# The opening of a written-out instruction order, exchanged for another

## The chip, the cores and the metric

The kernel runs on one core of a Trainium2 chip. The metric is the device time of one execution in microseconds (us). A core has TensorE (PE, matmuls; PEld is its weight load), VectorE (DVE), ScalarE (ACT), GpSimd (POOL) and SyncE (SP), which here does nothing but issue transfers. Each engine works its own instructions in program order, and waits at semaphores for the others.

## The reference, cut to what matters

A recurrence over 768 steps with a 40x40 state for each of 4 batches and 8 heads, and behind it an MLP with a quick GELU over the 3072 tokens of its output. All is float32.

```python
for t in range(S):                       # r, k, v, w, a, b: (4, 8, 768, 40)
    y[:, :, t] = einsum('bhd,bhde->bhe', rt, state)
    Sa = einsum('bhde,bhe->bhd', state, at)
    state = state * wt[:, :, None, :] - einsum('bhd,bhe->bhde', Sa, bt) \
            + einsum('bhd,bhe->bhde', vt, kt)
...
x = y.transpose(0, 2, 1, 3).reshape(3072, 320)
h = x @ w_in                             # 320 -> 2048
out = (h / (1 + exp(-1.702 * h))) @ w_out   # 2048 -> 320
```

## The kernel before

The 768 steps are cut in 12 chunks of 64, and the 4 batches in 2 pairs: 24 *units*, numbered in pairs, units 2c and 2c+1 being the two batch pairs of chunk c. Each unit is worked in the same stages. A name with a number is that stage of that unit (N0, N1):

- loads by SP: `logw`, `ak` (a and k side by side), `b`, `rv`, `RV`, `time`, and from unit 4 on `wc`. `ak`, `b` and `rv` are two transfers each, of 40 partitions; the others one of 128;
- the logarithm of the decay on ACT (L526), its sums over time on PE (`cum`, `cumc`), the exponentials FT, GT and G on ACT (L565 to L591), and a and b, k scaled with them (`ahT` L619, `bhT` L621, `khT` L624, `kh` and `bh` L627, on DVE or POOL);
- scores on PE: A and RV, and N, which needs ahT and bhT;
- the inverse of (1 - N), by five *levels* of squaring (`plain_level` for units 0 to 3): matmuls into `ps_level`, a copy of the result to PT (L784, "PT" or "PV") on ACT or DVE, a transpose to EX (L723) on DVE, then the next level. Behind the fifth a transpose (ES, L702), its spread into T (L707 on ACT, L709 on POOL), and two small steps Q and T21;
- the solution X, masked into M (L907, DVE), and y with the new state (`ps_y`, L934 to L945). For units from 2 on, the state of two units before enters (zr, zT, rz);
- x, y scaled by FT (L953), goes to DRAM and comes back turned as xT (L963, L967).

When both units of a chunk are done, its MLP follows: `up` (40 tasks of 8 matmuls in four groups, up0 to up3), GELU to g on ACT (L988), and `down` (2 x 8 tasks of 16 matmuls).

The MLP's weights come as 8 pieces of four transfers of 320 KB each (`wt0` to `wt7`; `extra`, part of `w_sb` or of `xT_all` hold them meanwhile), in a 64-bit form. One step on ACT (`rebased`, L447), three on DVE (L451, L455, L459) and one on POOL (L463, 3 us) turn a piece to float32. Pieces 0 to 3 serve up0 to up3, and 4 to 7 serve `down`. Piece 5 may be loaded when piece 0 is done, 6 after 3, and 7 after 5.

The work is kept as 2700 numbered tasks. No planner runs at build time: a string, `ORDER`, lists the tasks in the order in which they are issued, each as number, engine letter (p PE, a ACT, d DVE, g POOL, s SP) and, for work on PSUM, one of four bank pairs. `listed` reads it and checks each task's forerunners. Several tasks can run on either of two or three engines; the letter decides. What the order doesn't say, semaphores do: a task waits on its engine for its inputs and free buffers, and all behind it on that engine waits with it. That holds for SP too.

Of the kernel before, what the change touches and what calls it, by code (L numbers as in the profile page):

```python
# [58 lines left out]
class Plan:  # L59
# [29 lines left out]
    def listed(self, text):  # L89

        assert len(text.split()) == len(self.tasks)
        table, out, done = "exp", [], set()
        for one in text.split():
            e = next(e for e in ENGINES if ENGINES[e] in one)
            n, bank = one.split(ENGINES[e])
            t = self.tasks[int(n)]
            assert e in t.engines and t.after <= done and (e == "SP" or (t.pair is None) == (not bank))
            t.engine, t.bank = e, int(bank or 0)
            if e == "ACT" and t.table:
                t.load, table = t.table != table, t.table  # L100
            done.add(t)
            out.append(t)
        return out
# [4 lines left out]
0s 8s 26s 5s 7s 9s 3a 6s 87p0 88p1 24s 89a1 1s 2s 12s 102a 95d 100p2 90a0 93d 158a 101d2 98p3 96g 10s 94d 17s 97g 16s 99d3  # L108
103p1 4a 11s 132p0 104a1 105d1 142p2 143p3 133a0 106d 130p1 14s 144a3 13s 107p0 15s 18s 151g 108a0 109d0 51s 131a1 110p3 27s
149g 150d 111a3 112d3 159p0 156p1 145a2 161d0 160a0 152g 113p3 345s 92a 162d 25s 153d 114a3 163p2 42s 115d3 34s 19a 274s 264p0  # L110
165d2 265p3 164a2 22d 266a3 166p2 20d 273s 21d 33s 43s 167a2 154p3 168d2 23g 35s 28a 157d1 116p2 155d3 169p1 117a2 118d2 267a0
279d 63s 280g 119p3 277s 171d1 36s 44s 123a3 120d3 343s 125d3 121a 278g 124d3 29d 287a 126p2 170a1 288p0 127a2 30d 172p1 479s
122a3 31d 289a0 128p2 54s 173a1 45s 129d2 32g 62s 174d1 134p3 37a 290d0 175p2 344s 135d3 180a2 146s 178a2 275s 176d2 136p1
179a2 38d 181a2 39d 177a 282g 276s 291d 91s 138a1 182p0 188p3 281d 183a0 186p2 139d 137a1 283p0 187a2 184p1 189a3 40d 140s
292p2 46a 60s 284d0 41g 285p3 185d1 148a 286d3 190p0 293a2 294d2 334p1 335p3 357a 191d0 141s 268g 147s 336a3 315d 192p2 47d
337a1 348d 316p0 194a2 346s 295p3 349d 61s 317a0 195g 347s 358p1 296a3 297d3 360d1 318a0 298p3 271a 361d 319p0 338g 300d3 196s
193a2 320a0 355p2 385d 270s 48d 299a3 362p0 356d2 351g 301p3 363a0 364d0 350g 386p2 197s 302d3 365p0 387a2 269s 352g 359a1
303d3 388a2 323p1 367d0 366a0 321p3 49d 324a1 304p2 322a3 478s 325d1 50g 353p0 309a2 470p3 354d0 209p1 307a2 210p1 310a2 305d2
211p1 308a2 272d 198p0 341a 199p0 72s 212p1 70s 64a 200p0 340s 368p2 52s 342d 339s 69s 201p0 369a2 202p0 370d2 203p0 471a
213p1 65d 214p1 389p2 66d 472a3 483g 204p0 390a2 560s 371p3 67d 306a 53s 215p1 71s 482s 216p1 372a3 217p1 476a 220p2 373d3 68g  # L120
218p1 221p2 477d 219a1 205p0 222p2 206p0 223p2 224p2 78s 559s 207p0 55a 311p3 225p2 79s 312d3 80s 226p2 208a0 58d 313p1 374p3
314d1 227p2 56d 379a3 228p2 229p2 57d 326p0 230a2 59g 393p1 327d0 378a3 391p2 394a1 375d3 231p0 558s 392d2 376a 232p0 233p0
395d1 81s 73a 234p0 480s 381p2 235p0 474s 328p1 475s 382a2 74d 377a3 485d 380a3 236p0 75d 481s 492a 242p2 486d 243p2 82a 76d
484d 77g 383p3 237p0 384d3 244p2 329d1 330d1 488p3 473d 238p0 531d 245p2 487g 246p2 489d3 85d 532p1 708s 239p0 533a1 396p3
331d 534a1 240p0 247p2 397d3 332s 241a0 562s 535p1 83d 490p3 536a1 84d 398p0 706s 572a 491d3 86g 550p1 253p3 399d0 551a 555s
400d0 561s 333s 254p3 401d 255p3 552a1 564d 493p0 402s 556a 567g 570p1 554s 494d0 248p2 705s 563d 566g 249p2 495d0 498d 256p3
571d1 565g 403s 250a2 496a0 251d2 696p1 497g 557d 539p0 252s 537p2 257p3 538a2 704s 540d0 701s 258p3 553d 611d 697a 499d 573p2
259p3 576a2 574d2 784s 710d 700s 260p3 787s 541d0 575d2 404p0 578d 261a3 577g 405p0 579d 698a1 568p2 711g 500p1 406p0 569d2
501a1 407p0 262d3 580p2 702a 502d1 263s 408p0 582d2 409p0 503d 410p0 583d 504a 612p3 411p0 584g 613d3 412p0 614d3 413p0 505p1
709d 414a0 426p3 506d1 427p3 428p3 507d1 429p3 699d 581d2 430p3 615p1 703d 431p3 616a1 785s 585p0 432p3 508d 586a0 433p3 587d0  # L130
434p3 509a 588d 435p3 589d 448p2 436a3 510p1 590p0 511a1 449p2 592d0 591a0 512d1 415p3 513d 416p3 593d 514a 417p3 594g 418p3
515p0 419p3 516a0 517d0 595p1 518d 420p3 596a1 597d1 421p3 598d 422p3 519a 599d 423p3 424p3 520p0 425a3 437p1 521d0 438p1
523d0 522g 439p1 524d0 440p1 525d0 441p1 442p1 526d0 527p3 718p0 528a3 443p1 719d0 929s 444p1 720d0 529p3 445p1 721d0 446p1
530d3 600p0 723d 447a1 542p3 722d 724g 603d0 605a0 619p1 604d0 543d3 450p2 620a1 606d0 544p3 621d1 601d0 602d 617p1 707s 546d3
451p2 618a1 783s 712d 547g 713d 607p0 725p1 608a0 452p2 609p0 453p2 548s 610d0 932s 454p2 727d1 726d1 622p0 728d 545d3 729a
775p1 455p2 623d0 780s 776a 549s 756d 730p3 624p0 456d2 457d2 731d3 458s 459p2 777a1 778g 732d3 786s 788g 781a 779s 626d0
460p2 625d0 627g 733d 795p1 835d 734a 461p2 735p3 791g 462p2 628s 736a3 796d1 737d3 716p0 792g 738d 463p2 782d 739g 1011s
920p1 757p3 925s 464p2 717d0 758a3 629s 759a3 790d 465p2 740p0 789d 466p2 741a0 742d0 921a 797p3 467d2 760p0 1008s 468d2 800a3
923d 652p2 469s 761d0 922a1 653p2 926a 930s 798d3 714p1 799d3 654p2 924s 802d 801g 655p2 934d 803a 656p2 836p0 657p2 715d1
658p2 659p2 837d0 762p3 838d0 927d 660p2 763a3 661p2 764p1 662a2 743d 630p0 744d 928s 631p0 632p0 765d1 804p3 766d1 633p0  # L140
805a3 806d3 634p0 807d 635p0 808a 745p2 636p0 748d2 637p0 749d2 839p1 933g 750d2 638p0 840a1 1009s 751d2 639p0 809p3 746d2
935g 640a0 641p1 810d3 642p1 793p2 747a 811d3 674p0 812d 794d2 813a 752p3 643p1 753a3 814p2 644p1 815a2 816d2 754p3 645p1
755d3 646p1 817d 647p1 818a 767p2 841p3 768d2 648p1 842a3 649p1 819p2 650p1 820a2 821d2 769p3 822d 651a1 823d 675p0 771d3 931s
770d3 772g 824p2 936d 676p0 827a2 828a2 942p1 829a2 677p0 1153s 830a2 937d 945a1 773s 663p3 825d2 664p3 943d1 1156s 826a 665p3
944d1 999p2 947d 946g 666p3 1000a 1004s 980d 940p1 948g 667p3 941d1 668p3 774s 669p3 670p3 831p1 671p3 1001a2 1002d 1003s
832d1 672p3 1005a 1013d 678p0 673a3 1006d 833p2 843p1 679p0 834d2 1007s 844d1 938p2 845d1 680p0 939d2 846p3 681p0 847d3 949p1
1012g 682d0 848p2 950a1 683d0 1014d 684s 685p3 849d2 1015g 1010s 850d2 1021p0 1016g 951d1 686p3 1024a0 1232s 851d 1235s 981p2
687p3 982a2 952d 852s 1022d0 983a2 953g 1144p1 1023d0 688p3 1026d 1145a 1149s 1025d 1027g 984p2 1059d 689p3 1154s 954p0 853s
985a2 1147g 690p3 1158d 1148s 955a0 956d0 986p2 1146a1 957d 1150a 691p3 958d 987a2 1151d 988p0 692p3 989a0 1152s 990d0 959p1
693a3 865p2 960a1 694d3 866p2 961d1 867p2 695s 962d 868p2 963d 1028p0 869p2 1029a0 1030d0 870p2 1031d 1157g 871p2 1159d 1032a  # L150
1060p3 872p2 873p2 1061a3 874p2 1062d3 1033p1 875a2 854p0 1035d1 855p0 1036d 856p0 1037d 1063p3 857p0 1064d3 1034a1 858p0
964p2 859p0 965a2 966d2 1038p1 967d 860p0 1039a1 1040d1 861p0 1041d 1017p3 968a 1042g 862p0 1018d3 863p0 969p2 864a0 876p1
970d2 877p1 972d2 971g 1043p3 973d2 878p1 1044a3 974d2 879p1 975d2 880p1 881p1 1045d3 1019p0 1046d 976p2 1047a 882p1 1020d0
1233s 883p1 977a2 1166p3 884p1 1169a3 1167d3 1377s 978p0 885p1 1168d3 898p2 1171d 1170g 886a1 979d0 887p3 1172a 1048p0 991p1
1051a0 888p3 1052a0 992d1 889p3 1053a0 890p3 1054a0 891p3 1049d0 993p1 1050a 1067p0 994d1 1160g 1155s 892p3 1161d 1068a0 893p3
894p3 1069d0 1380s 895p3 1204d 1065p0 995d1 896p3 996d 1066a0 1231s 1055p1 899p2 897a3 1056d1 997s 1173p0 1223p3 900p2 1174a0
# [973 lines left out]
```

## Time and profile before

| | |
|---|---|
| times of three runs | 684.27, 674.71, 680.40 us; median 680.40 |
| profiled execution | 682.79 us, its span 681.1 us |
| granted clock of PE, mean | 0.99 |
| busy, share of the span | PE 96%, DVE 65%, ACT 49%, POOL 26% |
| transferred | 69.73 MB, of which 21.63 MB in the first 100 us |

The span runs from the first to the last instruction; 1.7 us lie around it. A row of the timeline gives start, length, engine, source line, operation, what it writes and reads, and in square brackets the idle time of the engine before it with what ended that. L300 is the helper of all matmuls, so matmuls are told apart by their PSUM tile: `ps_N`, `ps_level`, `ps_y`, `ps_up`.

### The profile page before, as it was taken

Reading aid. Unit: us, or ns where it says so; the run is one execution under the profiler, and the core shown is the slowest. Engines: PE = TensorE matmul, PEld = TensorE weight load, DVE = VectorE, ACT = ScalarE, POOL = GpSimd, SP = SyncE. Lnnn points to the kernel's source line nnn. Section 1 sums busy time; section 2 is a strip of 40 time slices with the busy share of each in tenths; the row PEclk is TensorE's granted clock in tenths of the full one; section 3 lists DMA queues with packets and bytes.
Section 4 is the critical chain, followed back from the end, with each engine's and each line's share of the span. In section 5 each row is a group of like instructions: output and inputs, shape, how many; then the busy total and the mean of one; then the engine's idle time right before and its main releaser. Section 6 shows DMA issues by size and latency. Waiting matters only on the chain.

```text
span 681.1 us, 42181 instructions
## 1 busy us (share of the span) xinstructions
PE 652.0 (96%) x19488; PEld 572.4 (84%) x19488; DVE 445.5 (65%) x906; ACT 330.7 (49%) x688; POOL 176.7 (26%) x204
## 2 busy tenths in 40 slices
PE   5777999999999999999999999999999999999997
PEld 5667888997987788888888898899899799889996
DVE  4687877777867668767776587868556766675001
ACT  4675845544564654664545445455454354252110
POOL 5443444225123123123123211321412421300000
PEclk9788999999999999999999999999999999999999
DMA  7874755205314314432404413513502312200100
GB/s 235 275 244 148 228 158 173 89 14 155 108 50 139 103 45 125 124 108 67 121 23 131 140 34 107 154 33 106 149 29 71 121 51 58 58 13 23 51 12 21
DMA packets 35312, 69.73 MB, mean 102 GB/s; under 512 B 5440, under 2 KB 14656, under 8 KB 35136
## 3 DMA queue, kind: packets, MB, share of 16 engines
q1 hardware_dynamic: 35136, 67.03, 32.8%
q8 instruction: 153, 2.51, 1.6%
q14 instruction: 23, 0.19, 0.1%
HBM read 59.15 MB, written 7.86 MB: 98 GB/s over the span
## 4 chain that ended last, share of the span: by engine, by line
PE 91%; DMA 4%; ACT 1%; DVE 1%; issue 1%; SPq 0%; ACTq 0%; DVEq 0%
PE ps_up L300 31%; PE ps_down L300 30%; PE ps_level L300 9%; PE ps_y L300 5%; PE ps_B L300 4%; PE ps_X L300 2%; PE ps_N L300 2%; PE ps_rz L300 2%; PE ps_RV L300 2%; PE ps_A L300 1%; DMA ak<-in_ak 1%; PE ps_zT L300 1%; PE ps_Q L300 1%; DMA time<-in_time 1%; PE ps_T L300 1%
## 5 line engine op out<-in xcount | busy, mean ns | idle before, releaser
L300 PE MATMUL ps_up<-xT_all,w_sb 64*64 64x256 f32 x3840 | 254.4, 377 | 2.0 <-DMA xT_all<-x_dram 1.1
L300 PE MATMUL ps_down<-w_sb,g 64*64 64x320 f32 x3072 | 240.3, 430 | 1.1 <-issue 0.9
L300 PEld LDWEIGHTS ps_up<-xT_all,w_sb 64*64 64x64 f32 x3840 | 172.9, 133 | 17.7 <-issue 2.5
L300 PEld LDWEIGHTS ps_down<-w_sb,g 64*64 64x64 f32 x3072 | 143.3, 133 | 31.4 <-issue 1.6
L988 ACT ACTIVATE g<-ps_up 128x1024 f32<-128x1024 f32 x48 | 49.1, 1024 | 44.7 <-PE ps_up L300 44.3
L709 POOL TENSOR_TENSOR EX<-ES,quads 128x512 f32<-128x512 f32 x29 | 38.3, 1323 | 115.5 <-DVE ES L702 83.1
L751 ACT COPY W<-ps_level 128x512 f32<-128x512 f32 x56 | 32.7, 585 | 69.1 <-PE ps_level L300 67.4
L300 PEld LDWEIGHTS ps_level<-W,EX 64*64 64x64 f32 x2560 | 59.2, 134 | 5.8 <-DVE T L830 0.2
L300 PE MATMUL ps_level<-W,EX 64*64 64x64 f32 (+1 forms) x2560 | 56.2, 217 | 0.0
L753 DVE TENSOR_TENSOR E<-two,ps_level 128x256 f32<-128x256 f32 x80 | 33.1, 415 | 34.7 <-ACT W L751 30.7
L707 ACT ACTIVATE EX<-ES,quads 128x256 f32<-128x256 f32 x80 | 36.3, 501 | 30.4 <-DVE ES L702 29.9
L619 POOL TENSOR_TENSOR ak<-ak,FT 128x512 f32<-128x512 f32 x16 | 22.0, 1378 | 76.2 <-DMA ak<-in_ak 54.4
L300 PE MATMUL ps_level<-PT,EX 64*64 64x64 f32 (+2 forms) x1280 | 34.9, 244 | 5.7 <-DVE EX L723 4.8
L300 PEld LDWEIGHTS ps_level<-PT,EX 64*64 64x64 f32 x1280 | 32.6, 145 | 8.9 <-DVE EX L723 5.7
L702 DVE STREAM_TRANSPOSE ES<-E 128x256 f32<-128x256 f32 x80 | 35.2, 442 | 4.7 <-DVE E L753 0.5
L300 PE MATMUL ps_y<-M,bh 64*64 64x104 f32 (+1 forms) x768 | 34.8, 247 | 1.3 <-DVE M L907 0.8
L300 PE MATMUL ps_y<-RV,kh 64*64 64x104 f32 (+1 forms) x768 | 34.9, 247 | 0.3 <-DVE EX L723 0.3
L891 ACT COPY B<-ps_B 128x416 f32<-128x416 f32 (+1 forms) x34 | 16.5, 492 | 33.5 <-PE ps_B L300 33.2
L300 PEld LDWEIGHTS ps_y<-RV,kh 64*64 64x64 f32 x768 | 28.9, 133 | 2.0 <-DVE M L907 0.5
L907 DVE TENSOR_TENSOR M<-ps_X,later 128x832 f32<-128x832 f32 (+1 forms) x24 | 23.8, 993 | 9.8 <-PE ps_X L300 9.5
L627 POOL TENSOR_TENSOR kh<-time,G 128x320 f32<-128x320 f32 x18 | 16.2, 902 | 48.4 <-PE ps_y L300 34.4
L300 PEld LDWEIGHTS ps_y<-M,bh 64*64 64x64 f32 x768 | 27.0, 133 | 1.9 <-DVE M L907 1.2
(131 smaller groups left out, 1097.2 us busy)
## 6 DMA issues: line engine op xcount, KB each, us to landing
ak<-in_ak SPq DMA_DIRECT2D x48, 160.0 KB
rv<-in_rv SPq DMA_DIRECT2D x48, 160.0 KB
time<-in_time SPq DMA_DIRECT2D x24, 320.0 KB
xT_all<-x_dram SPq DMA_DIRECT2D x48, 160.0 KB
wc<-in_wc SPq DMA_DIRECT2D x20, 264.0 KB
logw<-in_w SPq DMA_DIRECT2D x24, 160.0 KB
RV<-in_v SPq DMA_DIRECT2D x24, 160.0 KB
b<-in_b SPq DMA_DIRECT2D x48, 80.0 KB
```

The lines of the kernel that those rows point to most:

```text
L300: nc.tensor.matmul(o, lhsT, rhs, start=start, stop=True, skip_group_check=True)
L619: plan.add(R, {"DVE": 690.0, "POOL": 1270.0, "sbuf": True}, lambda t: of(t.engine).tensor_mul(ahT(), ahT(), FT_of(i)), reads=T("ak", "FT") ...
L627: plan.add(R + 4, {"POOL": 870.0, "DVE": 490.0, "sbuf": True}, lambda t, n=n, dst=dst: of(t.engine).tensor_mul(dst(i)[:, :, :D], by_head(t ...
L702: plan.add(rank, dve(256), lambda t: nc.vector.transpose(ES(n), source(t)), writes=[key("ES", n, 6)], **reads)
L707: nc.scalar.activation(dst[:, :, h], ES(n), ACT.Copy, scale=quads[:, h, :1])
L709: of(t.engine).tensor_mul(dst, ES(n).unsqueeze(2).to_broadcast([128, 8, 2, 32]), quads.unsqueeze(1).to_broadcast([128, 8, 2, 32]))
L751: plan.add(rank, any2(512), lambda t: copy(t.engine)(tiles_of(W(n + 1)), blocks(psum(t, ""), 64)), writes=[key("W", n + 1, 5)], pair=pair)
L753: plan.add(rank, dve(256), lambda t: nc.vector.tensor_sub(tiles_of(E(n + 1)), every(two32, [128, 2, 4, 32]), blocks(psum(t, ""), 64)[:, :, ...
L891: plan.add(R, any2(4 * wide), lambda t: copy(t.engine)(dst(), some(psum(t, "")[:, :, :208])), writes=[("Bv", i)] if x and c > 0 else T("B" ...
L907: plan.add(R + 1, dve(8 * wide), lambda t: nc.vector.tensor_tensor(M_of(i)[:, :, :wide].rearrange("p (j b) n -> p b j n", b=2), some(psum( ...
L988: plan.add(-45, {"ACT": 1030.0, "table": "gelu"}, lambda t: nc.scalar.activation(g_of(c * NQ + q).rearrange("p m r n -> p r m n"), psum(t, ...
```

## The change

`ORDER` is exchanged for another list of the same 2700 tasks, and `listed` stores for SP's tasks an attribute `window`, which nothing else reads. Matmuls, copies and transfers are the same in number and shape. The lists differ in their first parts: the first 163 of PE's 1080 tasks, and the first 95 of SP's 268. Behind that each engine has its tasks in the same order, with bank pairs 0 and 2 exchanged. 37 tasks have another engine: DVE has 796 tasks for 785, ACT 418 for 433, POOL 138 for 134.

```diff
             assert e in t.engines and t.after <= done and (e == "SP" or (t.pair is None) == (not bank))
             t.engine, t.bank = e, int(bank or 0)
+            if e == "SP":
+                t.window = t.bank
...
-0s 8s 26s 5s 7s 9s 3a 6s 87p0 88p1 24s 89a1 1s 2s 12s 102a 95d 100p2 90a0 93d 158a 101d2 98p3 96g 10s 94d 17s 97g 16s 99d3
-103p1 4a 11s 132p0 104a1 105d1 142p2 143p3 133a0 106d 130p1 14s 144a3 13s 107p0 15s 18s 151g 108a0 109d0 51s 131a1 110p3 27s
-149g 150d 111a3 112d3 159p0 156p1 145a2 161d0 160a0 152g 113p3 345s 92a 162d 25s 153d 114a3 163p2 42s 115d3 34s 19a 274s 264p0
...
+0s 6s 9s 5s 1s 17s 3a 7s 158a 87p2 102a 88p1 10s 89a1 8s 15s 16s 90a2 94d 4a 93d 18s 95d 103p1 97d 143p0 11s 96d 104d1 142p2
+14s 105d1 100p3 43s 144a0 106d 27s 98p1 101d3 145a2 107p0 149g 99d1 132p1 274s 109d0 151g 108d0 2s 19a 24s 42s 110p2 150d
+133a1 22d 26s 159p1 111a2 130p0 20d 154p3 131a0 161d1 273s 112d2 160a1 269s 162d 113p0 12s 155d3 114a0 25s 153d 163p3 152d 92a
...
```

The beginning of three engines' lists by name (Ln.m is level m of unit n; the number behind `wt` is the piece):

| engine | before | after |
|---|---|---|
| SP | logw0, RV0, wt1, ak0, rv0, time0, b0, wt1, logw1, logw2, rv1, ak1, wt0, wt0, b1, time1, RV1, wt0, wt0, wt4, wt1, rv3, wt1, wt3, wt2, b2, ak2 | logw0, b0, time0, ak0, logw1, wt0, rv0, ak1, RV0, wt0, wt0, wt0, b1, time1, wt3, wt1, b2, logw2, wt1, wt3, wt1, ak2, wc5, rv1, wt1, wt2, RV1 |
| PE | cum0, cumc0, RV0, A0, N0, B1 of 0, cum1, cumc1, B0 of 0, L0.0, L0.1, N1, RV1, L0.2, L1.0, cum2, cumc2, L1.1, A1, L0.3, L1.2, L0.4, Q0, N2, L1.3, T21 of 0, X0, L1.4, y0 | cum0, cumc0, N0, cumc1, cum1, RV0, A0, L0.0, B1 of 0, L0.1, N1, B0 of 0, A1, L0.2, L1.0, cumc2, cum2, L0.3, L1.1, L0.4, RV1, L1.2, Q0, N2, T21 of 0, L1.3, X0, L1.4, y0 |
| ACT | log0, FT0, preset, G0, preset, log1, P21 of 0, B1 of 0, FT1, PT, B0 of 0, PT, G1, P21 of 1, log2, PT, rebased0, PT, FT2 | log0, preset, preset, FT0, G0, log1, FT1, G1, rebased0, B1 of 0, PT, B0 of 0, P21 of 1, PT, log2, FT2, PT, G2, PT |

Further on, the last quarter of `wt2` has moved on SP from the 25th place to the 49th, behind the load of RV3, and `rebased2` on ACT from the 32nd place to the 53rd. The scaling of k and a for unit 1 stands first on POOL. T of units 0 and 1 is spread on POOL instead of ACT, and the copies to PT are on DVE for L0.0 and L1.0.

## The prediction

> **What bounds the kernel now.** I read the page's busy shares first, then a table of stretches, then the rows of single engines in the first 70 us, then the waits of SyncE's queue.
>
> ```profile
> span 681.1 us, 42181 instructions
> PE 652.0 (96%) x19488; PEld 572.4 (84%) x19488; DVE 445.5 (65%) x906; ACT 330.7 (49%) x688; POOL 176.7 (26%) x204
> ...
> PEclk9788999999999999999999999999999999999999
> ```
>
> TensorE is the bound: 29.1 us of the span are without a matmul, and the granted clock is below full only in the first slices. Where those 29.1 us lie (columns: stretch, length, busy time of PE, PEld, DVE, ACT, POOL, clock, DMA share, GB/s):
>
> ```profile
> 0.00:10.00 10.00, 3.44 (x90) 3.09 (x94) 4.62 (x10) 4.14 (x13) 7.92 (x41) 1.00 0.74 216
> 10.00:20.00 10.00, 7.46 (x210) 6.57 (x202) 4.23 (x7) 4.03 (x13) 4.50 (x4) 0.96 0.89 272
> 20.00:30.00 10.00, 8.10 (x260) 7.46 (x256) 6.80 (x11) 7.02 (x17) 1.56 (x2) 0.70 0.77 263
> 30.00:40.00 10.00, 6.49 (x224) 5.87 (x224) 7.57 (x14) 6.05 (x15) 6.43 (x4) 0.83 0.91 291
> 40.00:50.00 10.00, 7.61 (x324) 6.71 (x328) 9.37 (x17) 8.34 (x21) 4.02 (x3) 1.00 0.73 226
> 50.00:60.00 10.00, 6.57 (x288) 5.84 (x283) 7.17 (x13) 6.54 (x19) 3.90 (x8) 1.00 0.68 204
> 60.00:70.00 10.00, 9.67 (x372) 9.32 (x372) 7.01 (x11) 6.03 (x15) 5.58 (x4) 0.83 0.31 89
> 70.00:100.00 30.00, 28.41 (x754) 24.57 (x750) 23.58 (x33) 20.53 (x39) 12.14 (x6) 1.00 0.64 200
> 100.00:600.00 500.00, 497.97 (x15323) 429.09 (x15319) 353.18 (x742) 249.84 (x511) 129.66 (x138) 1.00 0.32 92
> ```
>
> Up to 60 us PE works 39.67 of 60 us: 20.3 us idle. From 60 to 600 us it idles 3.9 us, and the rest is the tail. The order of the first 60 us therefore decides 20.3 us and no more, plus what the clock takes. The score of unit 0 (32 matmuls) lasts 1.13 us at 11.53, the same shape 0.67 us at 55.83: the opening runs partly at half speed. The granted clock is half at 19.1 to 26.0, 36.2 to 39.6 and 60.1 to 63.5, and by the rows' lengths also before 15.7 (no record there). That is about 20.8 us of PE work at half speed, longer by some 37% (0.72 for 1.12 in the sums of logs): 7.7 us. All that can be won is 28 us (4.1%); over 2% (about what a measurement of this kernel can tell from no change) would need half of it.
>
> What PE waits for in there:
>
> ```profile
> 11.53 1.13 PE L300 MATMUL ps_N<-b,ak 40*64 40x64 f32 x32 [0.84 <-DVE b L621]
> ...
> 18.58 1.08 PE L300 MATMUL ps_level<-PT,EX 64*64 64x96 f32 x32 [1.69 <-DVE EX L723]
> ...
> 36.28 0.70 PE L300 MATMUL ps_Q<-T,P 64*64 64x64 f32 x16 [1.95 <-ACT T L707]
> ```
>
> ```profile
> 17.27 1.27 POOL L624 TENSOR_TENSOR ak<-ak,GT 128x512 f32<-128x512 f32 x1 [5.28 <-DMA ak<-in_ak]
> 19.77 0.69 DVE L621 SCALAR_TENSOR_TENSOR b<-b,GT 128x512 f32<-128x512 f32 x1 [1.25 <-DMA b<-in_b]
> ```
>
> So two kinds of wait: the first inputs (b0, ak1, b1), and then the chain of one level (matmuls, copy to PT, transpose to EX, next matmuls), some 2.8 us long, of which PE fills only part with the other unit.
>
> **The change, part by part.** No task is added or removed. 37 tasks of the opening change engine: 18 from ACT and 5 from POOL to DVE, 5 from DVE to ACT, 9 to POOL. Durations: the PT copy is 0.80 us on ACT and 0.92 on DVE; T's spread 0.91 on ACT, 1.27 on POOL; the small Tc copies 0.21 on ACT, 0.23 on DVE. One copy to PT and the transpose after it never overlap in the rows (ACT 20.18 to 20.98, DVE from 21.02), so on one engine they cost 1.64 us for 1.55. Net, DVE gets about 2.3 us more work; in 0 to 100 us it is busy 67.2 us, so this lies beside its idle time. Cover gone, it would cost its 2.3 us. The list's two new lines store an attribute that nothing reads: 0.
>
> *Loads.* The landing records of the trace give a ladder for the order of before: 983 KB landed at 6.8, 1.31 MB at 8.7, 1.80 at 10.4, 2.46 at 12.0, 3.11 at 17.05, 3.44 at 17.9, 3.93 at 19.7. Then a load waits for the eighth before it. After, the second load is b0, which must wait for the clearing of b on DVE (ends 2.54); RV0 was issued at 1.28. I shift the ladder by 1.2 us. ak0 is the fourth load in both orders, now with b0 and time0 before it: 8.0 (was 6.8). b0, which PE waited for (10.4 in before), is ahead of it. ahT0 0.69 on DVE: the first score N0 starts at 8.75, for 11.53. **Lead 2.8.** Bounds: 1.6 (another 1.2 of shift) to 4.0 (none).
>
> *Next.* PE has cumc1, cum1, RV0 and A0 between N0 and the first level (each 0.8 to 1.1 at half speed), so L0 starts at 13.9, for 15.2: lead 1.3. b1 is behind 3.44 MB (was 3.93): 17.9 + 1.2 = 19.1, then 0.69 for b and N1 at 19.8, for 20.67: lead 0.9. On ACT rebased0 (1.39 us) now stands ahead of the next copy to PT, and waits for the last quarter of weight 0: 3.28 MB, 17.5 + 1.2 = 18.7. Rebased0 to 20.1, B1 0.51, PT 0.80: 21.4; DVE does N1's 0.69 until 22.0, EX 0.72: the third level starts at 22.75, for 22.53. **Lead about 0 at 23 us.**
>
> *Units 0 and 1.* From there unit 0 goes first. Third level 22.75, PT on ACT to 25.1, EX to 26.5 behind DVE's queue; fourth level 27.2 for 30.63; PT behind the three exponentials of unit 2 (2.0 us) to 29.5, EX 30.2, fifth level 30.25 for 33.41. ES 32.4, T on POOL (1.27) 33.7, Q0 33.75 for 36.28; X0 36.6 for 40.56; M 1.0, behind EX of unit 1; y0 39.4 for 42.06. Lead 2.7. Unit 1 waits behind: L5 31.95 (31.56 before), Q1 44.1 for 45.53, T1 47.2, X1 48.3 for 49.54, y1 ends 52.0 for 53.95. **Lead 2.0.**
>
> *Units 2 and 3.* Unit 2's first level starts at 42.95 (47.49), its second at 46.5 (54.93), as DVE now does its transposes earlier. After y1 come 14 tasks of 0.5 to 1.4 us on PE in both orders, among them two levels of unit 3, whose inputs (ak3 and b3 scaled) wait for FT3: N3 54.5 for 55.83. With those in line the first `up` starts at 65.7, for 69.01. **Lead 3.3.** The round trip of x through DRAM ends at 62.6 (x1 56.0, out 2.2, back 4.0), so it doesn't hold that start; nor did it in before (63.6 for 69.0).
>
> *From `up` on* PE works without gaps in before (idle 1.6 in 70 to 100 us, bound of the further gain); the same matmuls are left, so the lead stays. Weight 2 is ready late now: its last quarter stands on SP behind RV3, which waits for y1; its ScalarE step follows rz3, and POOL ends at 71.2 for a use at 73.8. That costs 0 while these 2.6 us last. Weights 4, 6 and 7 have margins of 9, 3 and 1 us by the same counting. From the 164th PE task the lists agree but for exchanged bank numbers 0 and 2: nothing.
>
> My steps leave out hand-overs of 0.02 to 0.1 us; the chain of waits shows 5.0% of its first 100 us as issue, and I take off 0.8 us for steps that I have more of. **Sum: 3.3 - 0.8 = 2.5 us.** The profiled execution took 682.8 (span 681.1 and 1.7 around it): 680.3. The three runs have a median of 680.4, 2.4 below it, so I predict 680.4 - 2.5 = 677.9.
>
> [...]
>
> **The rivals.**
> *1. More of the lead arrives.* Units 0 and 2 lead by 3 to 8 us; only unit 3's two levels in line before `up` keep it to 3.3. If FT3 comes earlier than I count, the lead at `up` is some 6, and with two half-speed stretches fewer (2 x 1.2) the gain is 8: 672.4. For it: 20 us of idle time. Against: DVE at 9.37 of 10 us in 40 to 50.
> *2. Slower: ACT is held by weight 0.* Rebased0 ahead of PT's copy waits for a load. In before the four quarters had landed by 22.5. Were it so late here, PT comes 3.8 us later, the lead of 2.5 is a loss of 1.3, and the gap in PE brings two more half-speed stretches (2.4): 684.1. It decides from a landing at 21.2 (18.7 + 2.5). For it: ak1 took 7.0 us from issue to landing. Against: 1.8 MB fewer stand ahead.
> [...]
> *3. The lead is given back.* PE gets ahead of the weights: 2.6 us of margin at weight 2 are used up, or DVE's 2.3 us more come into the chain. Then 680.4 + 0.2: 680.6.
>
> **How the numbers follow.** Forecast 0.42 (675 to 680 by itself), rival 1 0.22, rival 2 0.20, rival 3 0.16. Of rival 1, 0.07 lies beyond 2% (below 666.8: half of all that can be won); of rival 2, 0.07 above 694.0 (several loads late, each before another copy). Within 2%: 0.86. The three runs shown spread over 9.6 us, which is part of the range: 668 to 689.
>
> **What would show it.** N0 before 10 us; the third level near 22.7; unit 0's y before 40.5 and unit 1's y ending near 52; first `up` at 64 to 67; PE idle up to 60 us between 15 and 20 us. The prediction is wrong if ACT stands idle over 2 us for weight 0 while PE has nothing (rival 2), if the first `up` comes before 63 (rival 1), or if PE idles over 2 us between `up` and 130 us (rival 3).

## The result, and the profile after

The changed kernel took 685.42 us (median of 20 runs, 679.99 to 688.19), the kernel before 680.14 (20 runs, 674.71 to 684.27). The ratio is 1.0073, with a 95% interval of 1.0050 to 1.0096: some 5 us slower, where 2.5 us faster was forecast. The profiled execution took 686.43 us.

The page of the changed kernel: span, busy shares, granted clock in 40 slices, and one line of the DMA queues (packets, MB, share):

```profile
span 684.7 us, 42162 instructions
PE 651.6 (95%) x19488; PEld 567.6 (83%) x19488; DVE 447.5 (65%) x921; ACT 322.3 (47%) x662; POOL 181.1 (26%) x211
...
PEclk9879999999999999999999999999999999999999
...
q8 instruction: 153, 2.51, 1.5%
```

PE's busy time is that of before (652.0), so the 3.6 us by which this execution's span is longer lie in its idle time: 33.1 us for 29.1. The stretches, with the columns of the prediction's table:

```profile
10.00:20.00 10.00, 6.85 (x234) 6.18 (x235) 6.97 (x12) 3.89 (x12) 2.50 (x2) 1.00 0.99 288
20.00:30.00 10.00, 8.02 (x280) 7.27 (x280) 7.62 (x13) 4.94 (x15) 4.83 (x4) 0.83 1.00 277
30.00:40.00 10.00, 5.87 (x174) 5.14 (x175) 5.16 (x14) 4.57 (x8) 1.99 (x2) 0.70 0.87 276
...
60.00:70.00 10.00, 6.56 (x320) 5.96 (x311) 6.72 (x11) 5.97 (x12) 7.11 (x8) 1.00 0.57 168
```

The DMA share is 0.99 and 1.00 from 10 to 30 us (0.89 and 0.77 before): the new order of loads leaves the DMA engines no pause ("full rings" below stands for stretches like these). From 30 to 40 us PE does 174 matmuls (224 before), and from 60 to 70 us it works 6.56 of 10 us, where before it worked 9.67.

What PE waited for in the first 100 us, changed kernel (what it waited for, us in all, times, longest; "issue" means that nothing in the profile held it):

```profile
PE ps_RV L302 <- issue: 5.2, 3, 2.8
...
PE ps_rz L302 <- issue: 1.6, 1, 1.6
PE ps_B L302 <- issue: 1.0, 1, 1.0
PE ps_N L302 <- issue: 1.0, 1, 1.0
PE ps_y L302 <- issue: 1.0, 1, 1.0
PE ps_level L302 <- issue: 1.0, 1, 1.0
PE ps_level L302 <- DVE EX L725: 0.9, 1, 0.9
```

The same view of before:

```profile
PE ps_level L300 <- DVE EX L723: 4.8, 5, 1.7
...
PE ps_Q L300 <- ACT T L707: 3.2, 2, 2.0
...
PE ps_down L300 <- issue: 0.9, 1, 0.9
...
PE ps_rz L300 <- issue: 0.8, 1, 0.8
```

Summed over all rows of this view, before waited 19.0 us for data and 3.0 for "issue", together 22.0; after waits 14.3 for data and 11.9 for "issue", together 26.2. So the new order does what an order can do: PE waits 4.7 us less for data. It then loses 8.9 us more to waits that no semaphore explains. Two of them in the timeline of the changed kernel (start, length, what, number of matmuls, idle time ahead):

```profile
31.85 0.34 PE L302 MATMUL ps_RV<-rv 40*64 40x64 f32 x8 [0.42 <-ACT PT L786]
35.03 0.92 PE L302 MATMUL ps_RV<-rv 40*64 40x64 f32 x24 [2.84 <-issue]
...
68.38 0.56 PE L302 MATMUL ps_rz<-rv,zT 40*64 40x64 f32 x24
70.58 0.28 PE L302 MATMUL ps_rz<-rv,zT 40*64 40x64 f32 x4 [1.64 <-issue]
```

Each is in the middle of a task, whose inputs are there: in the first, 8 of 32 matmuls are done, and PE stops for 2.84 us. Counted from the first matmul of the program, the "issue" waits stand at matmuls 220, 473, 600, 726, 1108, 1236, 1362, 1489, 1617, 1744, 1872 and 2254: always a multiple of 127 apart, within 2. A matmul has a weight load (19488 of each on the page), so 127 of them are 254 instructions, and the line of queue q8, which the page calls `instruction`, says the same from the other side: 153 packets of 16.4 KB for 2 x 19488 instructions of PE, 255 in each. What one such packet stands for is called a block here; the breaks are at the blocks' ends. The records of q8 give the times: after PE has crossed into a block, the packet of the next one starts some 2.1 us later on the mean of the first 15 (some 1.2 before), at worst 4.9 us (crossing at 27.60, packet at 32.50), and PE, where it stood still, goes on mostly 2.4 to 2.9 us behind the packet's start. Before has such breaks too: its five "issue" waits of the first 100 us, 3.0 us in all, stand within 4 matmuls of a block's end. Counted by place alone (starts more than 0.3 us apart, within 6 matmuls of a block's end) it has 4.1 us of breaks, against 15.3.

### The profile page after: what moved, and what is told of

The parts are those of the page before. It is cut to its first block, busy times and chain, and to the rows that moved or that the text cites. A ratio compares the mean times of both kernels' runs of the same rounds, so it can differ in the third digit from the quotient of the medians.

```text
span 684.7 us, 42162 instructions
## 1 busy us (share of the span) xinstructions
PE 651.6 (95%) x19488; PEld 567.6 (83%) x19488; DVE 447.5 (65%) x921; ACT 322.3 (47%) x662; POOL 181.1 (26%) x211
## 4 chain that ended last, share of the span: by engine, by line
PE 92%; issue 2%; DMA 2%; ACT 1%; DVE 1%; SPq 0%; ACTq 0%; DVEq 0%
PE ps_up L302 31%; PE ps_down L302 30%; PE ps_level L302 9%; PE ps_y L302 5%; PE ps_B L302 5%; PE ps_X L302 2%; PE ps_RV L302 2%; PE ps_N L302 2%; PE ps_rz L302 2%; PE ps_A L302 1%; DMA rv<-in_rv 1%; PE ps_zT L302 1%; DMA b<-in_b 1%; PE ps_T L302 1%; PE ps_cum L302 1%
## 5 line engine op out<-in xcount | busy, mean ns | idle before, releaser
L302 PE MATMUL ps_up<-xT_all,w_sb 64*64 64x256 f32 x3840 | 251.8, 378 | 1.5 <-issue 1.1
L302 PEld LDWEIGHTS ps_up<-xT_all,w_sb 64*64 64x64 f32 x3840 | 171.6, 134 | 17.8 <-issue 3.2
L302 PEld LDWEIGHTS ps_down<-w_sb,g 64*64 64x64 f32 x3072 | 137.2, 133 | 35.1 <-ACT zr L871 0.4
L709 ACT ACTIVATE EX<-ES,quads 128x256 f32<-128x256 f32 x80 | 36.3, 501 | 33.3 <-DVE ES L704 32.7
L621 POOL TENSOR_TENSOR ak<-ak,FT 128x512 f32<-128x512 f32 x18 | 23.5, 1304 | 78.2 <-DMA ak<-in_ak 51.5
L704 DVE STREAM_TRANSPOSE ES<-E 128x256 f32<-128x256 f32 x80 | 35.4, 443 | 4.3
L893 ACT COPY B<-ps_B 128x416 f32<-128x416 f32 (+1 forms) x33 | 16.1, 491 | 33.5 <-PE ps_B L302 33.3
L302 PEld LDWEIGHTS ps_y<-RV,kh 64*64 64x64 f32 x768 | 29.1, 133 | 3.2 <-issue 1.2
L302 PE MATMUL ps_B<-RV,A 64*64 64x104 f32 (+1 forms) x768 | 28.3, 250 | 2.0 <-issue 1.0
L302 PEld LDWEIGHTS ps_B<-RV,A 64*64 64x64 f32 x768 | 25.0, 135 | 5.7 <-issue 1.2
```

The source lines that it names most:

```text
L302: nc.tensor.matmul(o, lhsT, rhs, start=start, stop=True, skip_group_check=True)
L621: plan.add(R, {"DVE": 690.0, "POOL": 1270.0, "sbuf": True}, lambda t: of(t.engine).tensor_mul(ahT(), ahT(), FT_of(i)), reads=T("ak", "FT") ...
L704: plan.add(rank, dve(256), lambda t: nc.vector.transpose(ES(n), source(t)), writes=[key("ES", n, 6)], **reads)
L709: nc.scalar.activation(dst[:, :, h], ES(n), ACT.Copy, scale=quads[:, h, :1])
L893: plan.add(R, any2(4 * wide), lambda t: copy(t.engine)(dst(), some(psum(t, "")[:, :, :208])), writes=[("Bv", i)] if x and c > 0 else T("B" ...
```

## The experiments

Theory A: PE works faster than its instructions come, most of all beside full rings. Theory B: the 37 tasks with another engine make DVE or POOL the slower chain. Theory C (the prediction's second rival): ACT is held by the step of weight 0. Each ratio is to runs of before on the same chip; these had medians from 680.1 to 683.3 us. "Breaks" are counted by place as above, over the first 2140 matmuls of the one profiled execution (in the two last rows over the 1916 that do the same work); "data" and "issue" are PE's waits in its first 100 us. As a count by place, the 4.1 of before hold two waits for data (1.7 us), and the 7.5 of e17 leave out one of 2.2 us just behind a block's end.

| kernel | median, before | ratio (95%) | breaks | issue | data |
|---|---|---|---|---|---|
| before | 680.14 | 1 | 4.1 | 3.0 | 19.0 |
| after | 685.42, 680.14 | 1.0073 (1.0050 to 1.0096) | 15.3 | 11.9 | 14.3 |
| e10_after_again | 688.70, 682.83 | 1.0090 (1.0059 to 1.0122) | 16.4 | 13.2 | 13.6 |
| e1_letters | 687.65, 680.42 | 1.0104 (1.0065 to 1.0144) | 13.5 | 10.9 | 16.6 |
| e2_loads_before | 706.70, 680.42 | 1.0394 (1.0351 to 1.0437) | 7.1 | 7.9 | 35.4 |
| e3_loads_after | 699.20, 680.42 | 1.0293 (1.0246 to 1.0339) | 3.7 | 1.5 | 37.1 |
| e4_shift | 688.58, 680.42 | 1.0119 (1.0079 to 1.0158) | 12.5 | 10.7 | 11.5 |
| e7_b_first | 683.74, 683.33 | 1.0016 (0.9988 to 1.0044) | 5.5 | 3.9 | 22.3 |
| e8_after_depth4 | 682.50, 683.33 | 1.0004 (0.9975 to 1.0033) | 10.2 | 8.1 | 18.4 |
| e9_before_depth4 | 686.11, 683.33 | 1.0041 (1.0014 to 1.0067) | 6.4 | 2.9 | 25.8 |
| e11_depth4_rv1 | 684.25, 682.83 | 1.0013 (0.9987 to 1.0039) | 11.8 | 10.1 | 16.1 |
| e12_depth4_rv1_w0 | 685.35, 682.83 | 1.0055 (1.0025 to 1.0085) | 8.7 | 6.6 | 18.4 |
| e13_depth3 | 694.94, 682.83 | 1.0186 (1.0137 to 1.0235) | 12.2 | 6.4 | 24.1 |
| e14_depth4_early | 685.66, 681.78 | 1.0066 (1.0030 to 1.0101) | 9.4 | 8.7 | 15.8 |
| e15_depth4_late | 685.16, 681.78 | 1.0053 (1.0026 to 1.0081) | 15.1 | 11.6 | 15.9 |
| e16_depth4_to90 | 684.03, 681.78 | 1.0044 (1.0015 to 1.0073) | 11.5 | 8.3 | 19.2 |
| e17_after_wide | 682.09, 682.33 | 1.0000 (0.9973 to 1.0026) | 7.5 | 7.0 | 16.2 |
| e18_before_wide | 685.76, 682.33 | 1.0054 (1.0030 to 1.0078) | 5.4 | 5.8 | 20.0 |

**The letters.** In `e1_letters` the order is the changed one and the 37 tasks have their old engines again, as here P21 of unit 0 and the first copy to PT:

```diff
-... 104d1 ... 108d0 ... 121g ... 177g ...
+... 104a1 ... 108a0 ... 121a ... 177a ...
```

> The changed order with the engine letters of before for all 37 tasks; the order of PE's tasks and of SP's loads stays the changed one. Theory A (PE's instruction stream: its blocks of 256 instructions come late beside full DMA rings): neither the loads nor PE's order is touched, so the breaks at PE matmuls 220, 352, 473, 600 and so on stay, about 13 to 16 us in the first 16 of them (15.4 now), first up at 72 to 75, time 684 to 688 (ratio 1.005 to 1.011). Theory B (DVE and POOL have become the slower chain by the 37 tasks): first up back at 68 to 70 and time 679 to 682 (ratio 0.998 to 1.003).

Measured: 1.0104, breaks of 13.5 us, first `up` at 72.05. The letters are not the cause; the changed ones are, if anything, the better ones. Theory B falls.

**The loads alone.** `e2_loads_before` has all of the changed order but SP's transfers in the order of before; `e3_loads_after` has before with the first 40 of SP's transfers in the changed order.

```diff
-0s 6s 9s 5s 1s 17s 7s 10s 8s ...   (SP's tasks of the changed order)
+0s 8s 26s 5s 7s 9s 6s ...          (SP's tasks of before)
```

> The changed order on PE, ACT, DVE and POOL, with the engine letters of the change, but SP's 268 transfers in the order of before. Theory A: the rings empty now and then as in before, the blocks come within about 1 us of being asked for, the breaks at the block ends fall from 15.4 us to 4 to 8, first up at 66 to 70 in spite of a later first score (11 to 12), time 677 to 682 (ratio 0.996 to 1.003). Theory B (letters): the loads don't matter, time 684 to 688. Theory C (ACT held by the step of weight 0 that stands early in its order): weight 0 comes later in this order of loads (22.5 against 17.8), so the hold grows by 2 to 4 us: 686 to 690.

> The order of before on PE, ACT, DVE and POOL with its own letters, but the first 40 of SP's transfers in the changed order, the rest as in before. Theory A: the rings are full without a break from 5 to 45 us, and the breaks at the block ends rise from 4.2 us to 9 to 15, first up at 70 to 74, time 682 to 688 (ratio 1.003 to 1.012). Theory B: 678 to 681, as the first score can start earlier and nothing else changes. Theory C: ACT takes the step of weight 0 late in this order, so nothing is held: 678 to 681 too.

Both missed, for theory A as well: 1.0394 and 1.0293. Neither list of loads fits the other list of work. The timeline of `e2_loads_before` on POOL, then PE, and of `e3_loads_after` on ACT:

```profile
45.25 1.26 POOL L626 TENSOR_TENSOR ak<-ak,GT 128x512 f32<-128x512 f32 x1 [13.22 <-DMA ak<-in_ak]
...
49.00 0.71 PE L302 MATMUL ps_Q<-T,P 64*64 64x64 f32 x16 [12.79 <-POOL T L711]
```

```profile
59.66 1.36 ACT L449 ACTIVATE w_sb<-w_sb 128x1280 f32<-128x1280 f32 x1 [11.09 <-DMA w_sb<-in_w_in]
```

In the first, T of unit 0 stands on POOL behind the scaling of k and a of unit 2, whose load comes 13 us late, and Q0 waits 12.79 us for T. In the second ACT is held 11.09 us by a step of a weight, with the next copies to Tc and T behind it. These two runs show what an engine's order is worth beside the wrong order of loads, and speak neither for theory A nor against it: with PE idle for data for 35 to 37 us, the blocks have time to come. In `e2_loads_before` all 7.1 us of breaks but 0.4 lie behind matmul 1360, where those waits are over.

**The stream shifted.** `e4_shift` puts 64 small matmuls ahead of the first score, where PE waits for a load anyway:

```diff
             ps = psum(t, "ps_N")
+            for n in range(32 if i == 0 else 0):
+                mm(ps[HALF[0], 0, 400:408], ident[HALF[0]], ident[HALF[0], :8], True)
```

> The changed kernel with 64 more matmuls (32 calls of 8 columns into unused columns of the tile of the first score), put ahead of the first score of unit 0, where PE waits for a load. Theory A: the breaks stay at the same places of the stream of PE matmuls (473, 600, 1108, 1236, 1362, 1489, 1617, each within 5) and so fall 64 matmuls earlier in the work: the long break of 3 us leaves the RV score of unit 1 for the level ahead of it or goes, and so does the one in rz of unit 3. Any theory by which a data wait or a neighbour on another engine makes the break: they stay in the same tasks, that is at 537, 664, 1172, 1300. Time 682 to 688 in both.

The breaks lie at matmuls 473, 601, 728, 854, 1108, 1236, 1364, 1490, 1617 and 1745 of the stream: where they were, and so 64 matmuls earlier in the work. In the timeline of this run they have left RV of unit 1 and rz of unit 3, and stand in X and the levels:

```profile
41.26 0.78 PE L302 MATMUL ps_X<-B,T 64*64 64x104 f32 x9 [3.27 <-issue]
...
67.50 0.34 PE L302 MATMUL ps_level<-PT,ident 64*64 64x128 f32 x4 [1.21 <-issue]
```

No data wait and no neighbour moves like this. The breaks belong to the instruction stream.

**The supply by itself.** `m1_blocks` has nothing but 1024 matmuls in each of five stages and the transfers beside them:

```python
for n in range(calls // 4):                 # 512 calls a stage
    for f, u in QUARTERS:
        ...
        nc.tensor.matmul(ps[HALF[u], f, o:o + cols], left[HALF[f], ...], right[HALF[f], :cols], ...)
```

> Leaves out the whole computation and measures PE's instruction stream by itself: five stages of 1024 matmuls each (512 calls, the quadrant pattern of the scores, zeros as data): A 64 columns with no transfers, B 64 columns beside 40 loads of 320 KB, C 64 columns beside 96 loads of 160 KB in 40 partitions, D 104 columns beside 40 loads of 320 KB, E 104 columns after them. Theory A: in A a block of 127 matmuls takes more than the 2.7 us that its matmuls alone need at full clock (32 in 0.67): 3 to 3.8 us, with a break at each block's end; in B and C the breaks grow, a block taking 4 to 6.5 us; in E (5 us of work in a block) there are hardly any breaks, in D a few. Rival (the breaks of the kernel have to do with its waits, not with the supply of instructions): A, B and C go at 2.7 us for 127 matmuls without a break, loads or none.

Stages A and B in the timeline of PE:

```profile
10.49 2.09 PE L71 MATMUL ps_A<-right,left 64*64 64x64 f32 x128 [1.45 <-issue]
14.50 2.09 PE L71 MATMUL ps_A<-right,left 64*64 64x64 f32 x128 [1.91 <-issue]
...
44.71 3.69 PE L71 MATMUL ps_B<-right,left 64*64 64x64 f32 x128 [4.11 <-issue]
50.91 3.52 PE L71 MATMUL ps_B<-right,left 64*64 64x64 f32 x128 [2.51 <-issue]
```

In A, with no other transfer, PE does 128 matmuls (256 instructions with their weight loads) in 2.09 us and then stands still: a block takes 3.45 to 4.0 us. Beside full rings (395 GB/s from 40 to 60 us, in B) it takes 5.4 to 6.2 us: the packet starts 2.8 to 3.8 us after the crossing instead of 1.0 to 1.6, and PE goes on 2.2 to 2.9 us behind its start in both. The granted clock is also lower there: 1.00 on the mean of A, 0.72 on that of B. Stage A takes 28.0 us and B 42.4, for the same matmuls. In C, beside loads of 160 KB, a block takes 3.7 to 5.9 us. The last two stages are no test of what I expected of them: SP issued the loads of C until 135 us, well into D (110 to 146 us), and those meant for D from 136 to 168, most of them in E. In D, beside loads of 160 KB, the first 479 matmuls of 104 columns had no break over 0.3 us; in E, beside those of 320 KB, PE stood still for up to 3.2 us at a block's end, so matmuls of 104 columns alone don't do away with the breaks.

**The depth of the rings.** `e8_after_depth4` issues a transfer of 32 bytes behind each of SP's transfers 9 to 60. A transfer waits for the eighth ahead of it (SP's 412 transfers in the trace of the changed kernel use eight semaphores in turn), so half of those eight carry 32 bytes:

```diff
     for t in tasks:
         t.fn(t)
+        if t.engine == "SP":
+            if 8 <= loads < 60:
+                nc.sync.dma_start(spare[:, 8 * loads:8 * loads + 8], w_d[0][:1, :8])
+            loads += 1
```

> The changed kernel, with a transfer of 32 bytes behind each of SP's transfers 9 to 60: SP keeps eight in flight, so half of them are now of no weight, and about half as many bytes queue ahead of a block of instructions. Theory A: the packet of a block starts 1 to 2 us after the crossing before it (2 to 4.9 us now between 20 and 45 us), the break of 3 us at matmul 600 shrinks to 0 to 1, the breaks in all from 15.4 to 7 to 12 us; first up at 70 to 72.5 if the loads still come in time, and the time 681 to 684. If the depth of the queues doesn't matter to the blocks: breaks as now, 685 to 688.

Measured: 1.0004, against 1.0073 and 1.0090 of the changed kernel. The packets start some 1.5 us after the crossing (some 2.1), and the long break at matmul 600 is gone. `e9_before_depth4` is the same edit to before.

> Before, with the same 32-byte transfers behind SP's transfers 9 to 60. Theory A: its breaks are 4.2 us in all, so there is little to win: 3 to 5 us of breaks, and the time 679 to 682 (ratio 0.998 to 1.003), or up to 686 where a load that PE waits for comes later through the shallower queue.

There it costs 0.4%: before has few breaks to lose, and its loads come later (waits for data 25.8 us for 19.0). `e14_depth4_early` (transfers 9 to 34), `e15_depth4_late` (35 to 60), `e16_depth4_to90` (9 to 90) and `e13_depth3` (two small transfers behind each) ask where and how much:

> The changed kernel with a 32-byte transfer behind SP's transfers 9 to 34 alone (issued between 8 and some 32 us; of loads, logw2, wt1 to wt3 and the inputs of units 1 to 3). If the 5 us are lost where the rings are full (15 to 45 us): nearly all of what e8 won is here, the time 0.999 to 1.003 of before, the breaks at matmuls 352 to 726 fall to 3 us or less in all, and those from 1108 on stay at 6 to 9. If they are lost in the dense stretch after 50 us: 1.005 to 1.010, as the changed kernel.

> The changed kernel with a 32-byte transfer behind SP's transfers 35 to 60 alone (issued from some 27 us to 55). If the 5 us are lost where the rings are full early: little is won, 1.004 to 1.009 of before. If they are lost in the dense stretch: 0.999 to 1.003, and the breaks from matmul 1108 on fall from 8 us to 3 to 5.

> The changed kernel with a 32-byte transfer behind SP's transfers 9 to 90 (to about 90 us). If the full rings count in every stretch: 1 to 2 us better than e8 (1.0004 there), 0.997 to 1.000, with breaks of 7 to 9 us in all. If the dense stretch after 50 us has its breaks without any full ring (3.5 to 4 us a block, as in stage A of m1): no better than e8, 1.000 to 1.004.

> The changed kernel with two 32-byte transfers behind each of SP's transfers 9 to 60, so that two or three large ones are in flight. Theory A: the packets of the blocks start 0.5 to 1.5 us after the crossing, breaks of 6 to 9 us in all; but SP needs about 1 us for each load, and the loads come later: waits for rv1, ak2 or weights of 3 to 10 us, time 1.000 to 1.015 of before. If only the depth counted: 0.995 to 1.000.

With the early part covered, the breaks before matmul 700 fall from 6 us to 1 to 3 (e8, e11 to e14, e16), without it they stay (5.6 in e15). The breaks after matmul 1050 stay at 7 to 10 us in all of them. In time neither half alone gives what both give, and the longer cover of e16 gives less than e8, but the intervals of all three touch that of e8. So the depth of the rings makes the early breaks, but taking them away wins between 0.1 and 0.9%, since part comes back as waits for data: these rise from 14 us to 16 to 19. At depth 3 a load and its two small transfers take SP about 1 us (an estimate from the rows of e8: 0.35 us for a load, 0.22 to 0.29 for each small one, some 0.04 between them), the waits for data are 24.1 us, and the whole is slower.

`e10_after_again` is the changed kernel once more, beside `e11_depth4_rv1` and `e12_depth4_rv1_w0` on one chip. In e11 the load of rv1 is moved ahead of nine others, because PE waited for it in e8 (2.1 us). In e12 the step of weight 0 stands later on ACT too:

```diff
-... 11s 14s 43s 27s 274s ... 12s        (SP: b1, time1, wt3, wt1, b2, ..., rv1)
+... 11s 14s 12s 43s 27s 274s ...
-... 145a 19a 133a 111a 131a 160a 114a   (ACT: G1, rebased0, B1, PT, B0, P21, PT; e12 alone)
+... 145a 133a 111a 131a 160a 19a 114a
```

> The changed kernel once more, beside the next three on the same chip: ratio to before 1.004 to 1.010, breaks at the block ends 12 to 17 us, first up at 72 to 75.

> The changed kernel with a 32-byte transfer behind each of SP's transfers 9 to 60 (as in e8_after_depth4), and the load of rv1 moved up on SP to stand behind time1 (24th place to 15th): in e8 PE waited 2.1 us for rv1 at 30 to 32. Theory A: that wait goes, but part of it comes back as breaks at the block ends, since PE then asks for its blocks sooner: first up at 67 to 69, time 0.994 to 1.001 of before. If the rule were that waits for data set the time: the whole 2.1 us, 0.993 to 0.997.

> As e11_depth4_rv1, and the step of weight 0 on ACT stands behind the two copies to PT and B of unit 0 that it was ahead of; its three steps on DVE and one on POOL stand later too. Theory C (ACT held by weight 0, the prediction's second rival): the third level starts 1 to 2 us sooner (21.47 in e8), first up at 66 to 68, time 0.991 to 0.998 of before. Theory A: PE takes its second and third block faster than they come, the lead is eaten up at matmuls 352 to 600, and the time is that of e11_depth4_rv1 within 1 us.

Ratio and breaks of e10 came as expected, its first `up` did not: 69.05, as early as in before. Its break then comes 8 matmuls later:

```profile
69.15 0.61 PE L302 MATMUL ps_up<-xT_all,w_sb 64*64 64x256 f32 x7
71.81 4.94 PE L302 MATMUL ps_up<-xT_all,w_sb 64*64 64x256 f32 x56 [2.06 <-issue]
```

In e11 the wait for rv1 is gone, waits for data fall from 18.4 to 16.1 us, and waits for "issue" rise from 8.1 to 10.1: the same idle time under another name, and the same time (1.0013). In e12 the third level starts at 20.84 instead of 21.45, but Q0 then waits 2.71 us for T, and the time is 1.0055, no better:

```profile
35.91 0.71 PE L302 MATMUL ps_Q<-T,P 64*64 64x64 f32 x16 [2.71 <-POOL T L711]
```

Theory C falls.

**Fewer instructions, same columns.** `e17_after_wide` and `e18_before_wide` halve the number of matmuls in A, RV, N (units 0 to 3) and rz (2 and 3), and double their columns; every second set of weights is left out, so the kernels compute other values. As here in N:

```diff
-            for f, u in product(BITS, BITS):
+            n = 2 if i < 4 else 1
+            for f, u in product(BITS, BITS[::n]):
...
-                    mm(ps[HALF[b], e, o:o + 64], ahT()[CHANNELS[e], j], b_of(i)[CHANNELS[e], j], o == 0)
+                    mm(ps[HALF[b], e, o:o + 64 * n], ahT()[CHANNELS[e], j], b_of(i)[CHANNELS[e], j:j + 4 * n - 3:4], o == 0)
```

> The changed kernel, where the scores A, RV and N of units 0 to 3 and the two reads of the state (rz) of units 2 and 3 use half as many matmuls of twice the columns: every second matrix of weights is left out and its neighbour takes its place, so these values of the result are others. 224 of some 1740 matmuls ahead of the first up go, 1.8 blocks of instructions; the columns and the writes stay. Theory A (the supply of instructions sets the pace in the changed order): its breaks fall from 15.5 us to 8 to 12 and the time by 2 to 6 us, to 0.999 to 1.005 of before. If the breaks only stand in for other waits that would take their place: the time falls by less than 1.5 us, 1.005 to 1.009.

> Before, with the same matmuls at half the number and twice the columns, with the same values left out. Theory A: its breaks are 4 us in all and data waits set its pace, so it gains 0 to 2.5 us (0.996 to 1.000), less than the changed kernel does, and the gap between the two orders shrinks from 0.8% to 0.6% or less. If all that counts is the number of instructions whatever the order: both gain the same, and the gap stays 0.7 to 0.9%.

The changed order gains all that it had lost: 1.0000. PE's busy time is the same (651.4 for 651.6 us). Its largest waits now:

```profile
PE ps_N L302 <- ACT logw L528: 4.8, 1, 4.8
PE ps_level L302 <- issue: 4.0, 3, 3.1
...
PE ps_zT L302 <- issue: 1.8, 2, 1.5
```

One long break is left, at matmul 472. Before doesn't gain; it loses 0.5%, which no theory expected. Its waits for "issue" rise from 3.0 to 5.8 us, as the ends of the blocks fall into other tasks, and those for data from 19.0 to 20.0: together 3.8 us, about what it loses. Why fewer instructions bring it more such waits I can't say. With the same instructions taken out of both, the changed order is now the faster one: the gap of 0.7 to 0.9% has turned round. None of the versions beats before by more than the measurement tells.

## Why the prediction was wrong

| step (us) | before | forecast | after | after again (e10) |
|---|---|---|---|---|
| N0 | 11.53 | 8.75 | 10.21 | 9.70 |
| first level of unit 0 | 15.2 | 13.9 | 13.95 | 13.72 |
| N1 | 20.67 | 19.8 | 19.90 | 20.57 |
| third level | 22.53 | 22.75 | 22.53 | 23.17 |
| fifth level | 33.41 | 30.25 | 30.51 | 29.70 |
| Q0 | 36.28 | 33.75 | 37.44 | 34.49 |
| y0 | 42.06 | 39.4 | 44.79 | 41.03 |
| end of y1 | 53.95 | 52.0 | 59.3 | 55.4 |
| N3 | 55.83 | 54.5 | 61.10 | 57.19 |
| first `up` | 69.01 | 65.7 | 73.68 | 69.05 |
| matmul 2140 | 86.2 | | 91.3 | 89.8 |

**Loads, and the next steps to the fifth level: right within 0.3 us in the first profile, but for N0.** The ladder put the landing of ak0 at 8.0; it landed at 9.21. N0 so started 1.46 us later than forecast, with a lead of 1.32, just outside the bounds given (1.6 to 4.0). That the first level came on time all the same is luck: from N0 to it I added up the lengths of overlapping rows, 5.15 us, and it took 3.74. `e7_b_first` tested that lead alone, with b0's load second in before:

```diff
-0s 8s 26s 5s 7s 9s 3a 6s ...
+0s 3a 6s 8s 26s 5s 7s 9s ...
```

> Before, with one edit: the load of b0 stands second among SP's transfers (was seventh). The first score waits for b0, so it starts at 10.0 to 10.5 (11.53 before). Theory A: what is won there is lost at the next waits, since the third level waits on ACT's order and the blocks of instructions come no earlier: first up at 68 to 70, time 678.5 to 681.5 (ratio 0.997 to 1.002). Theory of the prediction (an earlier first score is carried on to the first up): first up at 67 to 68, time 678 to 679.5.

It missed: RV0, which stands ahead of N0 on PE, waited 5.57 us for rv0, and N0 started at 15.41. Even so the time stayed (1.0016).

**"Units 0 and 1" is the step that failed.** From the fifth level at 30.51 to Q0 I counted T's chain on POOL, 3.5 us; it took 6.9. Between them stands RV of unit 1, whose 32 matmuls I had at their row's length. It broke for 2.84 us at the end of a block. The level behind it, forecast at 31.95, started at 35.73, and Q0 is behind that on PE, though T was ready at 34.20. **"Units 2 and 3"** failed in the same way: between y1 and the first `up` I counted 13.7 us (52.0 to 65.7), it took 14.4, with breaks in N3, RV3 and rz3 (1.0 to 1.6 us each), while y1 itself ended 7.3 us late. In the second profile of the same kernel (e10) the same steps fail by less: RV of unit 1 breaks for 1.84 us, y1 ends 3.4 us late, and the first `up` comes when it came in before. From 17 to 70 us that execution had one half-speed stretch, of 3.4 us, where the other had two, of 3.4 and 10.2 us. The lead forecast for `up`, 3.3 us, was in neither, and by matmul 2140, behind the next breaks, both are later than before, by 5.1 and 3.6 us.

The sum had no term for instructions at all. "So two kinds of wait", I wrote of the first 60 us, and took the shares of "issue" for hand-overs of 0.02 to 0.1 us. The rows were there, in the timeline of before:

```profile
58.69 0.30 PE L300 MATMUL ps_rz<-rv,zT 40*64 40x64 f32 x8
59.84 0.74 PE L300 MATMUL ps_rz<-rv,zT 40*64 40x64 f32 x24 [0.85 <-issue]
```

A task cut after 8 of 32 matmuls waits for no semaphore. An estimate from `m1_blocks`: the 12 blocks from matmul 93 to 1617 need 41 to 48 us at the 3.45 to 4.0 us of stage A, and 65 to 74 at the 5.4 to 6.2 us beside full rings; from the first score (matmul 40) to the first `up` (1736) the forecast left 57. So little room was there, and an order that takes waits for data away takes the time away in which blocks arrive, as in e11. That the gain of data waits was real, 4.7 us where I forecast 2.5 in all, is the part that was right.

**The clock.** I allowed 1.2 us for a half-speed stretch more or less, 36% of the 3.4 us of the two shorter stretches in before. No run shows this term, nor that a gap in PE brings such stretches, as the price of rival 2 has it; the two profiles of the changed kernel differ by one half-speed stretch of 10.2 us between 17 and 70 us, and have spans of 684.7 (after) and 684.6 (e10). (The prediction's "longer by some 37%" is misworded: 1.12 is 56% more than 0.72, and full speed would save 36% of it, 7.4 us of the 20.8, near the 7.7 written.) On the chip of e10 the mean granted clock over all runs was 0.988 for the changed kernel and 0.9925 for before. 0.0045 of 680 us are at most 3 us: up to half of the 5.3 to 5.9 us may be this, the rest idle time. In the profile the longest half-speed stretch, 34.1 to 44.3 us, begins while the break at 32.2 to 35.0 lasts; that one brings the other is argued, not shown. In e8 and e17 the clock is that of before (0.9925 and 0.992 for 0.991).

**Where the time won back lies.** By their medians e8 and e17 take away the whole loss. Their single profiles don't show it as idle time: over the whole span PE idled 29.1 us in before, 33.1 in after and 35.0 in e10, but also 33.3 in e8 and 32.6 in e17. What sets the profile of e8 apart is PE's busy time, 648.2 for 651.6 us in after, with 6.8 us at half speed ahead of 600 us for 17.1. So it is shown that the breaks are the ends of instruction blocks, that the changed order waits 8.9 us longer at them and that both edits against them bring the time back; that they bring it back as shorter breaks is argued.

**The rivals.** Rival 2's price (684.1) came near, its mechanism didn't happen: ACT did stand idle for weight 0,

```profile
17.92 1.36 ACT L449 ACTIVATE w_sb<-extra 128x1280 f32<-128x1280 f32 x1 [3.75 <-DMA extra<-in_w_in]
```

but with a landing at 17.8, below the 21.2 from which I let it decide, and the third level came at 22.53 as before; e12 moved the step away and won nothing. Rival 3 asked for idle time between `up` and 130 us and for weight 2; PE didn't wait for a weight. (In e10 it did idle there for 3.7 us, but at the ends of blocks.) Rival 1's larger lead didn't come. Of the signs named, in the first profile, N0 under 10 us, y0, y1, the first `up` and 15 to 20 us of idle time up to 60 us (it was 21.7) all failed; only the third level fit.

**Open.** How the 5 us, and what e8 and e17 win back of them, divide between idle time and clock; why before gets slower with fewer instructions; and the breaks of 7 to 10 us after matmul 1050, which no depth of the rings took away: only fewer instructions cut them (2.3 us in e17).

## What to carry to other kernels

Where PE runs short matmuls (64 columns and fewer in four quadrants), count its instructions as you count its columns: in m1_blocks 128 of them with their weight loads were 2.09 us of work and took 3.45 to 4.0 us, and 5.4 to 6.2 beside full rings. In e11 an order that took 2.3 us of waits for data away got 2.0 us more of "issue" for them, and the same time; "issue" rows in the middle of a task, a fixed number of matmuls apart (127 here), were the sign. Wider matmuls (e17), or fewer bytes in flight while the dense part runs (e8), helped then; in the order that was not short of instructions the same two edits cost 0.4 to 0.5%.

## What the runs showed of the hardware

- Queue q8 (`instruction`) moved 153 packets of 16.4 KB for PE's 2 x 19488 instructions, one for 127 or 128 matmuls with their weight loads. The packet of the next block started after PE had crossed into the present one: 1.0 to 1.6 us later with idle rings, 2.8 to 3.8 beside 40 transfers of 320 KB (m1_blocks), 4.9 at worst in the changed kernel. Where PE had to wait in m1_blocks, it went on 2.2 to 2.9 us behind the packet's start in either case; the shortest cycle of a block with such a wait was 3.45 us.
- Beside long waits for data it didn't show: in `e2_loads_before`, with 12.8 us of waiting for T, none of the blocks' ends up to matmul 1236 had a break over 0.4 us.
- A transfer of 32 bytes took SP 0.22 to 0.29 us to issue, one of 320 KB 0.35 (e8), and each takes one of SP's eight semaphores, which the trace shows in turn: small ones made the queue shallower, at 0.4% of loss where the queue wasn't the trouble (e9).
